# Another order table and an uneven split of the last tile in a fused attention and feed-forward kernel

## The chip, the cores and the metric

The kernel runs on one core of one Trainium2 chip. The metric is the device time of one execution in microseconds (us); lower is better. The core's engines have queues of their own: TensorE (PE) multiplies matrices, VectorE (DVE) and ScalarE (ACT) do elementwise work and empty the accumulation banks, GpSimd (POOL) here starts the loads, and SyncE (SP) starts the transposing DMAs and the stores. Each engine works its instructions off in the order in which they were written and waits for other engines by semaphores.

## The reference

Two stages, joined. A linear attention with a learned feature map, and a feed-forward layer with a squared ReLU over its output:

```python
def phi(x):                      # x: 8 batches, 8 heads, 576 tokens, 64 wide
    proj = einsum('bhsd,df->bhsf', x, w_phi)            # 64 -> 128 features
    proj = proj - max(abs(proj), axis=-1, keepdims=True)
    return concatenate([exp(proj), exp(-proj)], axis=-1)
q_p, k_p = phi(q), phi(k)
kv = einsum('bhsf,bhsd->bhfd', k_p, v);  z = sum(k_p, axis=2)
num = einsum('bhsf,bhfd->bhsd', q_p, kv)
den = einsum('bhsf,bhf->bhs', q_p, z)[..., None] + 1e-06
x = (num / den).transpose(0, 2, 1, 3).reshape(4608, 512)
h = maximum(x @ w_in, 0)                                # 512 -> 2048
out = (h * h) @ w_out                                   # 2048 -> 512
```

Inputs and output are float32; the kernel multiplies in bf16.

## The kernel before

The 4608 tokens are 36 tiles of 128. A batch gives four full tiles and 64 rows that share a tile with the next batch's. The feed-forward part works in 20 chunks: four of one tile, then sixteen of two (`CHUNKS`).

For every batch the kernel

- loads k, q and v with POOL's DMAs, which cast to bf16: a main part and a rest part each (L504, L514; in pieces at the start, L507 and L525),
- turns k and q, so that the 64 features of a head lie on the partitions. Batches 0 and 1 do it on PE (L661, L856) with copies out of the banks by ACT or DVE (L456, L458). Later batches do it by transposing DMAs that SP issues: main of 16 blocks at L594, rest of 2 blocks at L598,
- projects k (L690) and q (L891, L900) on PE, takes row maxima on DVE (L627, L937) and exponentials on ACT (L635, L930), and multiplies v with a row scale (L776),
- sums up kv and z on PE (L791, L796), copies them out (kvs), and computes numerator and denominator (num/den, L984, L992); DVE adds up the pieces (L1016, L1018), and divides (L1055), which gives xo,
- turns xo into xT: on PE and by a copy in batches 0 and 1, by SP's transposing DMAs after that (L1078 for a full tile, L1081 for half a shared one).

For every chunk follow the up-projection (hp, L1143, four groups of matmuls for each tile of a chunk), ReLU (hr, L1161 on ACT or L1163 on DVE), square (sq, L1171 or L1173), down-projection (op, L1199, four parts of four matmuls for each tile), a copy of the result to SBUF (ot, L456 or L458) and a store by SP (L1221, L1224). The last tile is computed, copied and stored in two halves of 256 columns each.

The order of all this is not the order of the loops. The loops only create 2034 numbered operations. `ORDER`, a table found by a search outside of the kernel, lists their numbers in the order in which they are written to the engines; a minus sign puts an operation that two engines can do on its second one. `Plan.order()` walks the table and hands out the slots of the buffers (eight PSUM banks, two slots for each of kin, qin, vin, kT and qT, five for xT, and so on); an operation that takes a slot waits for those that read it before. `WARM` says in front of which operations PE runs filler matmuls, in units of 128 columns. Figures such as the "out" and "out2" prices in `WIRE` were used by the search alone and emit nothing.

Three waits matter below. The transposing DMA of a batch's q can be issued once the slot of qT that it overwrites is free, that is after the last projection of the q two batches before. POOL holds the loads of a batch until the main transposes of k and q of the batch before have landed: it copies one element of each (`seen`, L1240). And a chunk's up-projection waits until the xT of all its tiles has landed.

The numbers of a few operations: 864 is the last projection of batch 4's q, with a projection of k in the same operation; 857 is a num/den step; 852 and 862 issue the two transposes of x for chunk 12, 1100 and 1102 the main and rest transposes of q for batch 6; 1683 is a store; 1723 is the first up-projection of chunk 12.

Of the kernel before, what the change touches and what calls it, by code (L numbers as in the profile page):

```python
# [120 lines left out]
)  # L121


WARM = {46: 14, 48: 2, 56: 10, 63: 3, 70: 9, 77: 36, 84: 2, 133: 34, 137: 24, 147: 10, 155: 3}


class Slots:
# [128 lines left out]
def kernel(  # L256
# [14 lines left out]
    DM, DF = moe_w_in.shape  # L271
# [7 lines left out]
    NT = B * S // P  # L279
# [25 lines left out]
    plan = Plan()  # L305
# [875 lines left out]
    def op_chunk(c):  # L1181
        hst, sq, o_h2 = h2_ops[c]
        t0 = sum(CHUNKS[:c])
        for tt in range(CHUNKS[c]):

            wide = DM // 2 if t0 + tt == NT - 1 else DM
            for c0 in range(0, DM, wide):
# [3 lines left out]
                for qu in range(OPN):  # L1191
                    key = O_KEY[c][OPN * tt + qu]
# [98 lines left out]
```

## Time and profile before

| | before |
|---|---|
| median of 3 runs | 358.52 us (358.02 to 358.96) |
| profiled execution | 357.22 us |
| span of its trace | 355.4 us |
| PE busy | 345.2 us, 97% |
| DVE busy | 299.0 us, 84% |
| ACT busy | 273.2 us, 77% |
| POOL busy | 61.4 us, 17% |

The span runs from the first to the last instruction of the trace; the time of the execution has some overhead around it. In the rows that follow, a group of instructions is named by its line, engine, operation and the tiles it writes and reads; a row of a timeline gives start, length, engine, and what ended the idle time before it. A row of the windows gives busy time and number of instructions of each engine within a stretch of the span, the clock granted to PE (1.00 is full), the busy share of the DMA engines and their rate. SPq rows are issues by SP's queue; a DMA's row in the chain gives its time from issue to landing.

### The profile page before, as it was taken

What the parts mean: (1) busy time and instruction counts of PE and PEld (TensorE: products, weight loads), DVE (VectorE), ACT (ScalarE), POOL (GpSimd) and SP (SyncE); (2) the same over time, 40 slices, a digit from 0 to 9 for tenths busy, and PEclk for the clock granted to TensorE, in tenths of its full rate; (3) what the DMA queues carried; (4) which work ended last, traced back from release to release, by engine and by line L of the source; (5) the groups of instructions that cost most, each with busy time, mean ns of one, the idle gap of its engine ahead of it and who ended that gap; (6) DMA issues with size and microseconds to landing.
All of it is one profiled execution on the core that took longest, in us unless ns stands there. A gap on an engine that the chain in (4) does not pass through costs nothing.

```text
span 355.4 us, 9650 instructions
## 1 busy us (share of the span) xinstructions
PE 345.2 (97%) x3910; PEld 239.5 (67%) x3910; DVE 299.0 (84%) x669; ACT 273.2 (77%) x604; POOL 61.4 (17%) x99
## 2 busy tenths in 40 slices
PE   8889999999999999999999969999999999999996
PEld 4469678676858585758685856666865767686474
DVE  6899989999999997779997978989996999759040
ACT  5998998798889869797889976688859698282061
POOL 9634250705200070004200330000000000000000
PEclk9999999999999999999999999999999999999999
DMA  8999999999992699339972599153203020210401
GB/s 130 185 200 203 195 207 175 137 184 145 110 163 75 111 146 183 91 62 153 163 107 77 93 192 141 30 92 81 48 15 120 18 74 10 54 46 0 120 30 59
DMA packets 92203, 39.31 MB, mean 111 GB/s; under 512 B 59712, under 2 KB 87680, under 8 KB 92160
## 3 DMA queue, kind: packets, MB, share of 16 engines
q0 software_dynamic: 42752, 18.09, 43.4%
q1 hardware_dynamic: 49408, 20.62, 28.2%
q8 instruction: 30, 0.49, 0.6%
q14 instruction: 13, 0.11, 0.1%
HBM read 36.73 MB, written 9.44 MB: 130 GB/s over the span
## 4 chain that ended last, share of the span: by engine, by line
PE 86%; DMA 4%; ACT 3%; DVE 3%; POOL 1%; issue 1%; POOLq 0%; DVEq 0%
PE bk L1199 34%; PE bk L1143 34%; PE bk L984 4%; PE bk L796 4%; PE bk L891 3%; DMA xT<-xo 2%; DMA vin<-in_v_dram 2%; PE bk L690 2%; PE bk L900 2%; ACT qph L930 1%; DVE va L776 1%; PE bk L791 1%; ACT kph L635 1%; PE bk L992 1%; DVE var L766 1%; DVE m L627 1%
## 5 line engine op out<-in xcount | busy, mean ns | idle before, releaser
L1143 PE MATMUL bk<-xT,win 128*128 128x256 bf16 (+1 forms) x1280 | 135.8, 262 | 2.9 <-DMA xT<-xo 2.8
L1199 PE MATMUL bk<-wout,h 128*128 128x512 bf16 (+1 forms) x592 | 135.5, 374 | 0.0
L1143 PEld LDWEIGHTS <-win 128*128 128x128 bf16 x1280 | 112.5, 98 | 19.3 <-DMA xT<-xo 3.0
L930 ACT ACTIVATE qph<-bk 128x512 bf16<-128x512 f32 (+1 forms) x160 | 80.5, 564 | 14.4 <-PE bk L900 14.4
L1199 PEld LDWEIGHTS <-h 128*128 128x128 bf16 x592 | 53.9, 98 | 53.6 <-issue 0.6
L635 ACT ACTIVATE kph<-bk 128x512 bf16<-128x512 f32 (+1 forms) x160 | 82.0, 577 | 7.4 <-PE bk L690 7.1
L1161 ACT ACTIVATE hr<-bk 128x512 bf16<-128x512 f32 x96 | 57.6, 604 | 26.2 <-PE bk L1143 24.2
L937 DVE TENSOR_REDUCE mq<-bk 128x4 f32<-128x512 f32 (+1 forms) x80 | 48.5, 628 | 6.1 <-PE bk L891 5.9
L627 DVE TENSOR_REDUCE m<-bk 128x4 f32<-128x512 f32 (+1 forms) x80 | 48.2, 629 | 3.0 <-PE bk L690 2.3
L1171 ACT ACTIVATE h<-hr 128x512 bf16<-128x512 bf16 x72 | 45.2, 640 | 2.3 <-DVE hr L1163 1.8
L776 DVE TENSOR_TENSOR va<-vin,em 128x512 bf16<-128x512 bf16 x64 | 41.0, 684 | 0.9 <-DMA vin<-in_v_dram 0.7
L1163 DVE TENSOR_SCALAR hr<-bk 128x512 bf16<-128x512 f32 x48 | 32.8, 686 | 6.2 <-PE bk L1143 5.7
L1173 DVE TENSOR_TENSOR h<-hr 128x512 bf16<-128x512 bf16 x72 | 29.7, 418 | 8.8 <-ACT hr L1161 8.4
L456 ACT ACTIVATE ot<-bk 128x512 f32<-128x512 f32 (+1 forms) x25 | 14.8, 593 | 23.0 <-PE bk L1199 22.9
L984 PEld LDWEIGHTS <-qph 128*128 128x128 bf16 x512 | 22.2, 98 | 7.2 <-issue 1.2
L1016 DVE TENSOR_TENSOR tmp<-bk,tmp 128x260 f32<-128x260 f32 x64 | 24.9, 418 | 1.0 <-PE bk L984 0.6
L1018 DVE TENSOR_TENSOR tmp<-bk,e 128x260 f32<-128x260 f32 x62 | 23.7, 417 | 1.9 <-PE bk L984 1.2
L984 PE MATMUL bk<-kvs,qph 128*128 128x65 bf16 x512 | 24.7, 194 | 0.4 <-DVE mq L937 0.2
L1055 DVE TENSOR_TENSOR xo<-tmp,rden 128x512 bf16<-128x512 f32 (+1 forms) x39 | 24.6, 630 | 0.4
L796 PE MATMUL bk<-va,kph 128*128 128x65 bf16 x512 | 21.4, 194 | 0.0
L796 PEld LDWEIGHTS <-kph 128*128 128x128 bf16 x512 | 20.1, 98 | 1.1 <-issue 0.3
L891 PEld LDWEIGHTS <-qT 64*128 64x128 bf16 x288 | 8.7, 94 | 12.1 <-issue 10.5
(70 smaller groups left out, 267.1 us busy)
## 6 DMA issues: line engine op xcount, KB each, us to landing
out_dram<-ot SPq DMA_DIRECT2D x31, 256.0 KB, 2.5
vin<-in_v_dram POOLq DMA_DIRECT2D x8, 512.0 KB, 9.6
kin<-in_k_dram POOLq DMA_DIRECT2D x7, 512.0 KB, 8.2
qin<-in_q_dram POOLq DMA_DIRECT2D x7, 512.0 KB, 10.9
win<-in_moe_w_in_dram POOLq DMA_DIRECT2D x4, 512.0 KB, 12.3
wout<-in_moe_w_out_dram POOLq DMA_DIRECT2D x2, 1024.0 KB, 15.8
out_dram<-ot SPq DMA_DIRECT2D x10, 128.0 KB, 2.4
xT<-xo SPq DMA_TRANSPOSE x36, 2.5
```

Source lines behind the costliest of these rows:

```text
L627: nc.vector.tensor_reduce(out=st["m"].rearrange("p (n c) -> p c n", c=2)[:, par, n0 : n0 + n], in_=st["pj", g, par][:, :n], axis=AX.X, op= ...
L635: nc.scalar.activation(out=st["kph"][:, s, n0 : n0 + n, par], in_=st["pj", g, par][:, :n], func=ACT.Exp, scale=1.0 - 2.0 * s)
L776: nc.vector.tensor_tensor(out=st["va"][:, s, gs, 0:D], in0=tiles["v", b].rearrange("p h i d -> p (h i) d")[:, gs, :], in1=st["em"][:, s, g ...
L796: nc.tensor.matmul(out=kv[:, at + n, :], lhsT=st["kph"][:, s, 2 * h + i // 2, i % 2, :], rhs=st["va"][:, s, h * NI + i, :], start=False, s ...
L930: nc.scalar.activation(out=of_bank(st["qph", pt][:, s], bank), in_=st["pq", pt, pi][bank][:, :w], func=ACT.Exp, scale=1.0 - 2.0 * s)
L937: nc.vector.tensor_reduce(out=of_bank(st["mq", pt], bank), in_=st["pm", pt, pi][bank][:, :w], axis=AX.X, op=ALU.max, apply_absolute_value= ...
L984: nc.tensor.matmul(out=st["nd", pt, half, s, ab or n // 4][:, n % 4, :], lhsT=qph[:, s, half, sl, :], rhs=kvs[:, s, sum_of(sl), :], start= ...
L1143: nc.tensor.matmul(out=hp[:, mi, :], lhsT=win[:, kc, mc * P : (mc + 1) * P], rhs=st_x[c][:, kc, 0:nt, :], start=kc == kcs[0] and (ab is No ...
L1161: nc.scalar.activation(out=out_, in_=in_, func=ACT.Relu)
L1163: nc.vector.tensor_scalar(out=out_, in0=in_, scalar1=0.0, scalar2=None, op0=ALU.max)
L1171: nc.scalar.activation(out=out_, in_=hr, func=ACT.Square)
L1199: nc.tensor.matmul(out=st["op"], lhsT=hst["h2"][:, mc, tt * P : (tt + 1) * P], rhs=wout[:, mc, cols], start=(mc == 0), stop=(mc == KC2 - 1))
```

## The change

`ORDER` and `WARM` are replaced by the result of another search, in which transposed k and q had to be ready a small reserve, and transposed x a larger one, ahead of their first use. The operations are the same 2034 up to the last tile's, and 179 of them are on another engine than before. The last tile is computed in a part of 384 columns and one of 128, in place of two of 256. The condition for the label "out" is rewritten so that the 384 columns have it.

```diff
 ORDER = (
...
-    917, 845, 847, 846, 915, 1680, 848, 849, 864, 850, 851, 1685, 865, 1100, 869, 922, 1677, 868, 1681, 870, 866,
-    923, -1686, 924, 1688, 921, 852, 867, -1687, 919, 1682, 857, 1691, 1689, 1102, 859, 858, 925, 1694, -1690, 860,
-    928, 1683, 871, 1692, 1697, 861, 1695, 1693, 920, 862, 1700, 1696, 1698, 927, 1103, 1703, -1699, 926, 931, 1701,
...
+    836, 1673, 837, 839, 838, 916, 1674, 840, 818, 842, 841, 1678, -1675, 917, 828, 913, 918, 854, 1676, 857, 843,
+    1679, 914, 855, 856, 915, 844, 858, 847, 859, 1680, 845, 846, 1681, 848, 849, 860, 1677, 850, 864, 861, 1682,
+    1685, 1100, 920, 922, 865, 867, 923, 1688, 919, 924, 851, 1686, 1691, 925, 1102, 870, -1687, 926, -1689, 871,
+    1694, 869, 1692, 852, 929, -1690, 1697, 935, 1695, 862, 927, 1700, -1693, 1698, 931, 1703, -1696, 930, 1683,
...
 )
-WARM = {46: 14, 48: 2, 56: 10, 63: 3, 70: 9, 77: 36, 84: 2, 133: 34, 137: 24, 147: 10, 155: 3}
+WARM = {46: 14, 54: 5, 56: 10, 63: 3, 70: 43, 77: 8, 84: 2, 133: 23, 137: 24, 147: 12, 171: 1}
...
-            wide = DM // 2 if t0 + tt == NT - 1 else DM
-            for c0 in range(0, DM, wide):
+            for c0, wide in [(0, 3 * DM // 4), (3 * DM // 4, DM // 4)] if t0 + tt == NT - 1 else [(0, DM)]:
...
-                plan.issue("hw", 1 + two, key, {"sp": (1.1, 1.1) if two else (0.4, 0.4)}, e_out, "out" if wide == DM else "out2", [o_ot],
+                plan.issue("hw", 1 + two, key, {"sp": (1.1, 1.1) if two else (0.4, 0.4)}, e_out, "out" if wide > DM // 2 else "out2", [o_ot],
```

The lines shown of `ORDER` are those around 864 and the transposes of q for batch 6 and of x for chunk 12. In SP's queue the issues there stand in the order 1100, 852, 1102, 1683, 862 before and 1100, 1102, 852, 862, 1683 after.

197 rows, old and new, of the table ORDER are left out of this document.

## The prediction

> **What bounds the kernel now.** I read the busy table first, then what TensorE (PE) waits for, then the same thing by stretches of the span, then the chain that ended last around the one long wait. The page's totals, and the one long entry among PE's waits (total us, times, longest):
>
> ```profile
> span 355.4 us, 9650 instructions
> PE 345.2 (97%) x3910; PEld 239.5 (67%) x3910; DVE 299.0 (84%) x669; ACT 273.2 (77%) x604; POOL 61.4 (17%) x99
> ...
> PE bk L1143 <- DMA xT<-xo: 2.8, 1, 2.8
> ```
>
> PE is busy for 345.2 of 355.4 us and xT stalled it once, for 2.8 us. The windows show where PE was not busy.
>
> ```profile
> core 0: us, PE busy (x) PEld busy (x) DVE busy (x) ACT busy (x) POOL busy (x), PEclk, DMA share, GB/s
> 15.00:20.00 5.00, 4.41 (x50) 2.64 (x49) 4.94 (x11) 4.46 (x14) 2.75 (x5) 1.00 1.40 199
> 20.00:27.70 7.70, 6.52 (x126) 4.86 (x124) 7.41 (x19) 7.47 (x20) 3.77 (x7) 1.00 1.40 198
> 27.70:208.00 180.30, 180.00 (x2194) 128.50 (x2193) 167.13 (x377) 158.30 (x355) 41.03 (x65) 1.00 0.96 140
> 208.00:211.00 3.00, 0.18 (x7) 0.06 (x2) 2.66 (x6) 1.48 (x4) 1.89 (x3) 1.00 1.60 169
> 345.10:352.30 7.20, 7.14 (x50) 4.62 (x48) 1.12 (x2) 1.62 (x4) 0.00 (x0) 1.00 0.15 55
> 352.30:355.40 3.10, 0.00 (x0) 0.00 (x0) 0.00 (x0) 0.36 (x1) 0.00 (x0) 1.00 0.12 42
> ```
>
> Until 27.70 no engine has much to spare: VectorE (DVE) is busy 4.94 of 5.00 and 7.41 of 7.70 us, ScalarE (ACT) 7.47 of 7.70. From 27.70 to 208 PE runs without loss and DVE is at 167.13 of 180.30, 93%. Then comes the hole of three microseconds, and the end costs 3.1 us after the last matmul. The granted clock is 1.00 in every window. So time can come from three places only: the start, the hole, the tail; and what the table moves elsewhere is hidden unless it makes a new hole.
>
> The hole, in the chain of waits:
>
> ```profile
> 202.97 8.00 DMA xT<-xo
> ...
> 211.02 1.05 PE bk L1143 x8
> ```
>
> The second transposed x of chunk 12 is issued at 202.97, lands 8.00 us later, and PE starts 0.05 us after that. The transposes of x usually land much faster (DMA to landing, 36 of them):
>
> ```profile
> DMA to landing us min/median/max: 2.3/2.5/8.9
> ```
>
> **The change, part 1: chunk 12.** The old order gives PE 8.65 us of work between the last num/den matmuls feeding this x (they end at 199.35, in the PE rows below) and the chunk's first up-projection, which is due at 208.0. The new order puts two up-projection groups, four down-projection groups, two kv groups and two num/den groups more between the same two operations: 8.65 + 6 x 0.88 + 2 x 0.60 + 2 x 0.25 = 15.6 (0.88 is 205.07 to 205.95, and eight matmuls of 256 columns take the same; the other two are read off below). Were the chain from producer to PE's start unchanged (199.35 to 211.02, 11.67 us), the hole would vanish. But the new order also moves x in SyncE's queue. The rows of that queue, with the two of POOL that start batch 7's loads:
>
> ```profile
> 196.38 1.91 SPq L594 DMA_TRANSPOSE qT<-qin  x1
> 198.39 1.65 SPq L1078 DMA_TRANSPOSE xT<-xo  x1
> 200.14 2.12 SPq L598 DMA_TRANSPOSE qT<-qrest  x1
> 202.35 0.53 SPq L1224 DMA_DIRECT2D out_dram<-ot  x1
> 202.97 1.89 SPq L1078 DMA_TRANSPOSE xT<-xo  x1
> ...
> 200.81 0.34 POOL L1240 COPY seen<-qT 1x1 bf16<-1x1 bf16 x1 [20.20 <-DMA qT<-qin]
> 201.27 0.90 POOL L504 DMA_DIRECT2D kin<-in_k_dram  x1
> ```
>
> The old queue has q main, x, q rest, out, x. The new one has q main, q rest, x, x, out. So neither x leaves before both transposes of q, and q main can leave only when the batch 4 projections have freed the q slot. In the PE rows those projections end at 196.32, just ahead of q main's issue at 196.38:
>
> ```profile
> 196.11 0.28 PE L690 MATMUL bk<-w,kT 64*128 64x128 bf16 x4
> 196.32 1.05 PE L1143 MATMUL bk<-xT,win 128*128 128x256 bf16 x8
> ...
> 198.94 0.41 PE L984 MATMUL bk<-kvs,qph 128*128 128x65 bf16 x8
> 199.19 5.40 PE L1143 MATMUL bk<-xT,win 128*128 128x256 bf16 x48
> ...
> 205.07 1.04 PE L1199 MATMUL bk<-wout,h 128*128 128x512 bf16 x4
> 205.95 0.22 PE L791 MATMUL bk<-var,kph 128*128 128x130 bf16 x1
> ...
> 206.55 1.03 PE L1199 MATMUL bk<-wout,h 128*128 128x512 bf16 x4
> ...
> 211.02 1.05 PE L1143 MATMUL bk<-xT,win 128*128 128x256 bf16 x8 [2.83 <-DMA xT<-xo]
> ```
>
> The real reserve is therefore counted from that release. Before: 196.32 to about 208.0, 11.68 us of PE work. After, between the same projections and the same chunk, the order has the same eight up- and three down-projection groups, two kv groups more (205.95 to 206.55, 0.60 each) and one num/den group less (198.94 to 199.19, 0.25): 11.68 + 1.20 - 0.25 = 12.63. On the old clock PE now wants x at 196.32 + 12.63 = 208.95. The queue delivers: q main 196.38, plus 1.91, 2.12 and 1.65 of issues with 0.10 between them, puts the second x at 202.36, only 0.61 earlier than before. With the same 8.00 and 0.05 it starts PE at 210.41, a wait of 1.46 us. Bounds: with the longest landing, 8.9, 2.36; if it lands at 210.97 as before, because batch 7's loads set the time and these still follow the landing of q main, 2.07; with the median landing, none. The 256 KB store that went out ahead of x now follows it, which should shorten the landing somewhat. I take a wait of 1.2, nearest to the 1.46 of the same transfer: the term is 1.2 - 2.83 = **-1.6** (-2.8 to -0.5).
>
> The Trainium skill's "DMA: Bandwidth & Descriptors", section "Queues, rings and completion order", says that a DMA engine takes turns between the queues it has work for, packet by packet. By that an x sharing with one load would take about twice 2.5 us, some 5 by estimate; the 8.00 of this trace is longer, so the row decides here, and the fair share stands below as a rival.
>
> **Part 2: the start.** Copies change engine. Up to the first up-projection DVE takes over w's copy, two casts of k, two copies of qT and two of kvs, and gives up one of xT and one of qT, each of 256 columns:
>
> ```profile
> L458 DVE CAST kvs<-bk 128x260 bf16<-128x260 f32 x11 | 4.6, 420 | 2.2 <-PE bk L796 2.2
> L458 DVE COPY qT<-bk 128x512 bf16<-128x512 bf16 x2 | 0.7, 414 | 0.0
> L458 DVE COPY xT<-bk 128x256 bf16<-128x256 bf16 x3 | 0.8, 280 | 0.0
> L458 DVE CAST kin<-h 128x256 bf16<-128x256 f32 x1 | 0.3, 295 | 0.0
> L458 DVE CAST w<-bk 128x128 bf16<-128x128 f32 x1 | 0.3, 291 | 0.8 <-PE bk L405 0.8
> ```
>
> That is 0.29 + 2 x 0.295 + 2 x 0.414 + 2 x 0.42 - 2 x 0.28 = 2.0 us more for DVE, on an engine that was 97% busy from 15 to 27.7; ACT loses more than it gains. The fillers in front of PE's operations are shifted and stay about as many (147 to 145 units of 128 columns); PE has idle time for them there. Bounds: +2.0 if DVE sets the start throughout; -0.6 if ACT does (PE lost 0.59 from 15 to 20). The first copies fall while DVE awaits loads, the others where it is full: **+0.6**.
>
> **Part 3: the middle.** Counted the same way over the rest, DVE gets about 2 us more; the cover is the 13 us that DVE had free between 27.70 and 208. The other chunks' reserves for x grow or stay ample, and none waited before (the one entry among PE's waits). A spot where DVE was already late may cost a few tenths: **+0.1** (0 to +0.8).
>
> **Part 4: the tail.** The last tile's 32 matmuls of 256 columns become 16 of 384 and 16 of 128.
>
> ```profile
> 27.74 1.05 PE L1143 MATMUL bk<-xT,win 128*128 128x128 bf16 x16
> 28.63 0.28 PE L856 MATMUL bk<-ident,qrest 128*128 128x128 bf16 x2
> ...
> L456 ACT ACTIVATE ot<-bk 128x256 f32<-128x256 f32 x2 | 0.8, 384 | 2.5 <-PE bk L1199 2.5
> ...
> out_dram<-ot SPq DMA_DIRECT2D x31, 256.0 KB, 2.5
> out_dram<-ot SPq DMA_DIRECT2D x10, 128.0 KB, 2.4
> ```
>
> From 27.74 to 28.63 sixteen of 128 take 0.89, 56 ns each; four of 512 take 0.88 (205.07 to 205.95), 220 each, and 256 about half of it, so 384 is about 165: 16 x (165 + 56) = 3.54 us against 32 x 110 = 3.52. No difference. The copy after the last matmul goes from 384 ns on ACT to about 291 on DVE (w's row), and the last store from 128 to 64 KB, by the step between the two rows 0.1 less: **-0.2** (-0.4 to +0.4, if 128 columns run slower here). The Trainium skill's "TensorE: Matmul & The Clock Gate", section "Back-to-back issue gap", gives about 81 ns for 128 columns in a stream of weight loads and matmuls, by which the tail would gain 0.4 less; the row of 56 ns contradicts it.
>
> **Sum.** -1.6 + 0.6 + 0.1 - 0.2 = -1.1. The profiled execution took 357.22, 1.8 us beside its span and 1.3 below the median of 358.52; it would take 356.1, and the median becomes 357.4. What a measurement here can tell from no change is 0.3%, 1.08 us, so the forecast lies right at that bound.
>
> **Rivals.** (a) The fair share: x lands within 6.5 us and the hole is gone. For: the median of 2.5, the store no longer ahead. Against: 8.00 in the same place. The Trainium skill's "DMA: Bandwidth & Descriptors" is the page whose rule would give it. -2.83 + 0.6 + 0.1 - 0.2 = -2.3, 356.2. (b) No gain: DVE sets the start and all of 2.0 appears. For: 4.94 of 5.00. Against: ACT is as full from 20 on and is relieved. -1.6 + 2.0 + 0.1 - 0.2 = +0.3, 358.8. (c) Slower: the queue holds x longer than the reserve grew. The transposes of q do not always issue in 1.91:
>
> ```profile
> L594 SPq DMA_TRANSPOSE qT<-qin x6: 1841/2430/3527, 57.7 to 236.5; - x6
> ```
>
> With 3.53 and a landing of 8.9 the wait is 1.46 + 1.62 + 0.9 = 3.98, 1.15 above the old; with the other terms +1.65, 360.2. The term turns into a loss once x lands over 9.4 us after 202.36. For: both x stand behind both q. Against: 1.91 is near the minimum of that row, in this very place. (d) More than that: (a) and a start that gains its 0.6, 355.0.
>
> **Chances and range.** Forecast 0.50 (its own range 356.3 to 358.4), (a) 0.17, (b) 0.15, (c) 0.13, (d) 0.05. Leaving out (c) and (d), 0.18, gives 355.8 to 359.4. Faster by over 1.08 us: (a), (d) and 0.28 of the forecast, 0.50; within: 0.22 of the forecast and 0.13 of (b), 0.35; slower: (c) and 0.02 of (b), 0.15.
>
> **What the new profile would show.** Part 1: SyncE's rows with both q transposes ahead of both x, the second x some 6 us after q main, and a PE wait on xT at chunk 12 of 1 to 2 us; none says (a), 3 or more (c). Part 2: the first row of L1143 with 128 columns, at 27.74 now, and PE's idle time up to 41 us; later by 2 says (b). Part 3: no other entry among PE's waits above half a microsecond. Part 4: the last down-projection to the end in about 0.2 us less. The prediction is wrong if a chunk other than 12 waits for x, or if the wait there is set by something that the old trace does not show.

## The result, and the profile after

The changed kernel takes 353.5 us (median of 4 executions, 353.32 to 354.35) against 358.52 us (358.02 to 358.96): a ratio of 0.9865, 95% interval 0.9844 to 0.9885. That is 5.0 us less, where 1.1 was forecast and 355.8 was the lower end of the range. The two profiled executions are only 2.9 us apart, 354.35 and 357.22: the one of before happened to be among its kernel's shorter ones, the one of after its kernel's longest. Both halves of this, the 2.9 and the other 2.1, need a reason.

The page of the changed kernel, and PE's waits in it (total us, times, longest):

```profile
span 352.6 us, 9652 instructions
PE 345.7 (98%) x3908; PEld 238.8 (68%) x3908; DVE 302.1 (86%) x678; ACT 268.9 (76%) x594; POOL 63.2 (18%) x100
...
PE bk L432 <- DVE zero L425: 1.0, 1, 1.0
PE bk L791 <- DVE mq L937: 0.6, 1, 0.6
PE bk L1095 <- DVE xo L1059: 0.4, 1, 0.4
```

PE is as busy as before, in a span 2.8 us shorter, and no wait for xT is left. The windows of the changed kernel say the same by stretches; the one around chunk 12 is the third:

```profile
core 0: us, PE busy (x) PEld busy (x) DVE busy (x) ACT busy (x) POOL busy (x), PEclk, DMA share, GB/s
0.00:27.70 27.70, 24.60 (x274) 13.98 (x274) 23.75 (x55) 20.30 (x51) 18.40 (x32) 1.00 1.21 170
27.70:204.00 176.30, 175.92 (x2128) 125.07 (x2127) 165.44 (x376) 151.16 (x337) 37.99 (x59) 1.00 0.95 139
204.00:212.00 8.00, 8.00 (x125) 5.85 (x124) 7.73 (x16) 7.01 (x20) 6.22 (x9) 1.00 0.99 140
212.00:342.00 130.00, 130.00 (x1340) 89.35 (x1335) 102.75 (x229) 88.79 (x186) 0.61 (x1) 1.00 0.32 66
```

SyncE's queue at chunk 12 has the order that was foretold, q main, q rest, both x, the store. POOL's rows are what was not:

```profile
198.24 1.93 SPq L594 DMA_TRANSPOSE qT<-qin  x1
200.27 1.61 SPq L598 DMA_TRANSPOSE qT<-qrest  x1
201.97 2.98 SPq L1078 DMA_TRANSPOSE xT<-xo  x2
205.04 0.53 SPq L1223 DMA_DIRECT2D out_dram<-ot  x1
...
204.26 0.43 POOL L1239 COPY seen<-qT 1x1 bf16<-1x1 bf16 x1 [25.91 <-DMA qT<-qin]
204.72 0.90 POOL L504 DMA_DIRECT2D kin<-in_k_dram  x1
...
DMA to landing us min/median/max: 2.5/2.7/3.0
```

The second x is issued at 203.69 (201.97 plus the first one's 1.67 and a gap) and the first load of batch 7 at 204.72. Before, that load came first, at 201.27, and the x at 202.97. The last line is the landing of the two x of chunk 12: 2.5 and 3.0 us in place of 8.00. PE begins the chunk, the last of these rows, without a wait; the first row is the one behind the projections that free the q slot:

```profile
198.17 6.29 PE L1143 MATMUL bk<-xT,win 128*128 128x256 bf16 x56
...
210.62 0.41 PE L796 MATMUL bk<-va,kph 128*128 128x65 bf16 x8
210.86 1.04 PE L1143 MATMUL bk<-xT,win 128*128 128x256 bf16 x8
```

The difference of the two spans can be split at the chunk's first row. Ahead of chunk 12 PE now has four down-projection matmuls of 512 columns more (0.88 us by the rows), four kv pairs of L791 and L796 more (0.30 each, as from 210.25 to 210.56 in the new trace) and two matmuls of 128 columns fewer (0.11): 2.0 us of work more. Without its wait of 2.83 the kernel before would have begun the chunk at 208.19, and with 2.0 more at 210.2; the changed kernel begins at 210.86, so it has lost 0.7 up to there. From there to the end of the last matmul it takes 138.4 us (to 349.23) against 141.2 (to 352.24), 2.9 less, 2.0 of which is the work moved: a gain of 0.9. After the last matmul it takes 3.4 against 3.2. So -2.8 for the hole, +0.7, -0.9, +0.2: -2.8.

### The profile page after: what moved, and what is told of

It reads as the page before. It is cut to its first block, busy times and chain, and to the rows that moved or that the text cites. A ratio compares the mean times of both kernels' runs of the same rounds, so it can differ in the third digit from the quotient of the medians.

```text
span 352.6 us, 9652 instructions
## 1 busy us (share of the span) xinstructions
PE 345.7 (98%) x3908; PEld 238.8 (68%) x3908; DVE 302.1 (86%) x678; ACT 268.9 (76%) x594; POOL 63.2 (18%) x100
## 4 chain that ended last, share of the span: by engine, by line
PE 94%; DVE 3%; ACT 2%; issue 0%
PE bk L1143 36%; PE bk L1198 35%; PE bk L796 4%; PE bk L984 4%; PE bk L891 3%; PE bk L690 2%; PE bk L900 2%; PE bk L432 2%; ACT kph L635 1%; PE bk L791 1%; DVE m L627 1%; PE bk L992 1%; PE bk L856 1%; PE bk L1095 1%; DVE mq L937 1%; DVE va L776 0%
## 5 line engine op out<-in xcount | busy, mean ns | idle before, releaser
L1198 PE MATMUL bk<-wout,h 128*128 128x512 bf16 (+2 forms) x592 | 135.7, 374 | 0.0
L1161 ACT ACTIVATE hr<-bk 128x512 bf16<-128x512 f32 x94 | 56.4, 601 | 20.8 <-PE bk L1143 20.2
L1171 ACT ACTIVATE h<-hr 128x512 bf16<-128x512 bf16 x73 | 46.2, 638 | 5.6 <-DVE hr L1163 4.7
L1163 DVE TENSOR_SCALAR hr<-bk 128x512 bf16<-128x512 f32 x50 | 34.1, 685 | 4.3 <-PE bk L1143 2.5
L456 ACT ACTIVATE ot<-bk 128x512 f32<-128x512 f32 (+1 forms) x22 | 13.3, 604 | 20.0 <-PE bk L1198 19.9
L984 PEld LDWEIGHTS <-qph 128*128 128x128 bf16 x512 | 21.4, 98 | 6.0 <-issue 1.2
L984 PE MATMUL bk<-kvs,qph 128*128 128x65 bf16 x512 | 23.8, 194 | 0.5 <-DVE mq L937 0.3
L796 PE MATMUL bk<-va,kph 128*128 128x65 bf16 x512 | 21.3, 194 | 0.0
L796 PEld LDWEIGHTS <-kph 128*128 128x128 bf16 x512 | 20.1, 98 | 1.1 <-issue 0.2
L458 DVE COPY ot<-bk 128x512 f32<-128x512 f32 (+1 forms) x15 | 9.9, 661 | 9.4 <-PE bk L1198 9.3
```

The lines of the kernel that those rows point to most:

```text
L796: nc.tensor.matmul(out=kv[:, at + n, :], lhsT=st["kph"][:, s, 2 * h + i // 2, i % 2, :], rhs=st["va"][:, s, h * NI + i, :], start=False, s ...
L984: nc.tensor.matmul(out=st["nd", pt, half, s, ab or n // 4][:, n % 4, :], lhsT=qph[:, s, half, sl, :], rhs=kvs[:, s, sum_of(sl), :], start= ...
L1161: nc.scalar.activation(out=out_, in_=in_, func=ACT.Relu)
L1163: nc.vector.tensor_scalar(out=out_, in0=in_, scalar1=0.0, scalar2=None, op0=ALU.max)
L1171: nc.scalar.activation(out=out_, in_=hr, func=ACT.Square)
L1198: nc.tensor.matmul(out=st["op"], lhsT=hst["h2"][:, mc, tt * P : (tt + 1) * P], rhs=wout[:, mc, cols], start=(mc == 0), stop=(mc == KC2 - 1))
```

## The experiments

**A second trace of the kernel before.** No edit.

> The kernel before, unchanged, for a second trace. If the hole at chunk 12 is the same in every execution, PE waits for xT between 2.5 and 3.1 us there again and the span is 355 to 356. If the hole varies with how the transfers fall (which would explain that the profiled execution was 1.3 us below the median), the wait differs from 2.83 by 1 us or more and the span moves by as much.

It took 358.82 us, with a span of 357.0, longer than the 355 to 356 expected with the same wait. The wait is the same:

```profile
PE bk L1143 <- DMA xT<-xo: 2.9, 1, 2.9
```

but what follows the hole is not. The windows of this second trace, around the hole:

```profile
205.00:208.00 3.00, 3.00 (x49) 1.98 (x44) 3.00 (x6) 3.00 (x9) 0.63 (x2) 1.00 1.41 213
208.00:211.00 3.00, 0.19 (x7) 0.07 (x3) 2.68 (x6) 1.49 (x4) 1.87 (x3) 0.99 1.50 191
211.00:212.00 1.00, 0.90 (x5) 0.65 (x6) 0.00 (x0) 0.00 (x0) 0.26 (x1) 0.50 1.58 185
212.00:213.00 1.00, 1.00 (x8) 0.75 (x7) 0.00 (x0) 0.00 (x0) 0.00 (x0) 0.50 1.58 185
213.00:214.00 1.00, 1.00 (x20) 1.00 (x19) 0.00 (x0) 0.97 (x3) 0.00 (x0) 0.50 1.31 174
214.00:215.00 1.00, 1.00 (x23) 0.97 (x21) 0.52 (x2) 0.29 (x1) 0.00 (x0) 0.83 1.65 88
...
211.10 1.89 PE L1143 MATMUL bk<-xT,win 128*128 128x256 bf16 x8 [2.91 <-DMA xT<-xo]
```

The granted clock (the seventh figure) is at 0.50 when PE starts again at 211.10 and stays there for some 3.2 us; the first eight matmuls of chunk 12 take 1.89 us instead of 1.05. At half clock those 3.2 us hold 1.6 us of work less. In the trace that the prediction was made from, the same windows have 1.00. So the hole costs 2.9 us in some executions and about 4.5 in others.

The mean granted clock that is on record for every execution bears this out. In the four sets of executions of the kernel before that came with these experiments, each on another chip, 25 have a clock of 1.0 and 34 one of 0.995, which is what 3.4 us at a half come to. Their medians are 357.1 and 358.7 us in the first set, then 356.6 and 358.3, 357.3 and 358.7, 357.1 and 358.7: the lower clock goes with 1.4 to 1.7 us. Where in the span it fell, only a trace can show.

Why one hole brings the clock down and another does not can be argued from two traces. In all fourteen traces the stretches between two changes of the clock are whole multiples of 3.41 us long (204.80 and 3.41 in this one; 351.57 in the first trace, from 4.25 to 355.82). Counted in such steps, the hole nearly fills one step in this trace (first row) and straddles two in the first trace (the other rows):

```profile
207.51:210.92 3.41, 0.68 (x19) 0.56 (x17) 3.17 (x7) 1.98 (x5) 1.79 (x3) 1.00 1.47 212
...
205.64:209.05 3.41, 2.54 (x43) 1.74 (x40) 3.41 (x7) 3.41 (x10) 0.00 (x0) 1.00 1.56 208
209.05:212.46 3.41, 1.44 (x25) 1.35 (x26) 1.61 (x4) 0.79 (x2) 2.14 (x3) 1.00 1.51 170
```

How little work in a step is too little, these two do not tell. The Trainium skill's "TensorE: Matmul & The Clock Gate", section "What's actually happening", has the clock at a half after an idle window of some 3.4 us that runs freely, not from the kernel's start; a hole of 2.9 that brings the clock down in one execution and not in another agrees in kind, though the hole is shorter than that figure.

**The loads held back, old table.** POOL also waits for both x of chunk 12 before the loads of batch 7:

```diff
                 for n, name in enumerate("kq"):
                     nc.gpsimd.tensor_copy(out=seen[0:1, n : n + 1], in_=turned[name, b - 1][1][name + "T"][0:1, 0, 0:1])
+                if b == 7:
+                    for u in range(2):
+                        nc.gpsimd.tensor_copy(out=seen[0:1, u : u + 1], in_=st_x[12][0:1, 0, u, 0:1])
```

> The old table, but POOL also waits for both transposes of x for chunk 12 before it starts the loads of batch 7 (it copies one element of each). If these loads make the transpose take 8.0 us, it lands in 2.5 to 4.5, PE's wait there goes from 2.8 to 0 and the time falls by about 2.8 us (0.992); the loads start some 4 us later and nothing waits for them. If the store and the transposes on SyncE's own queue make it slow, it still takes over 6 us, the wait stays above 1 us and the time falls by 1.5 us at most.

354.12 us (353.96 to 354.95), 0.9893 of the kernel before (0.9869 to 0.9917). SyncE's and POOL's rows:

```profile
202.24 0.53 SPq L1224 DMA_DIRECT2D out_dram<-ot  x1
202.86 1.22 SPq L1078 DMA_TRANSPOSE xT<-xo  x1
...
205.50 0.41 POOL L1243 COPY seen<-xT 1x1 bf16<-1x1 bf16 x1 [2.32 <-DMA xT<-xo]
205.95 0.90 POOL L504 DMA_DIRECT2D kin<-in_k_dram  x1
```

The x leaves SyncE as late as before (202.86, behind the store and the q transposes) and lands by 205.5: 2.5 us, not 8.0. The loads of batch 7, and nothing on SyncE's own queue, made it slow. The gain, 3.7 us by medians, is more than the wait of 2.8: none of the six executions has the lower clock, and against the seven of the kernel before on this chip that do not have it either (median 357.1) the gain is 3.0. Three more lines in the old table give as much as the new table with the old tail on the same chip (354.18, below).

**The hole filled.** In the old table, 12 fillers of 512 columns ahead of the first up-projection of chunk 12, in the bank that it overwrites:

```diff
                     kcs = range(KC1) if ab is None else (ab, ab + 2)
+                    for _ in range(12 if c == 12 and mcs[0] == 0 else 0):
+                        nc.tensor.matmul(out=hp, lhsT=zero, rhs=zero.unsqueeze(1).to_broadcast([P, 4, P]), start=True, stop=True)
```

> The old table, with 12 filler matmuls of 512 columns (some 2.6 us) in front of the first up-projection of chunk 12; they write the bank that the real matmuls overwrite and do not wait for x. The hole is as long as before, but PE is busy in it. If a hole of 3 us lets the clock fall to a half afterwards in some executions (as in the second trace of the kernel before) and this makes the spread of 356.1 to 359.4, the executions now lie within 0.8 us of each other, near 356.5 to 357.2, and their median is 0.5 to 1.5 us below that of the kernel before. If the spread has another source, it and the median of about 358 stay.

357.09 us (356.61 to 358.58, 12 executions) against 358.18 (355.75 to 359.48, 17), a ratio of 0.9987 (0.9965 to 1.0008). The interval includes 1, but the clocks on record decide: none of the twelve has the lower clock, while eleven of the seventeen of the kernel before have it (358.02 to 359.48; the other six take 355.75 to 357.03). The three longest of the twelve, 357.71, 358.42 and 358.58, have spans of 355.8, 355.6 and 355.4 us, close to the others' 354.8 to 355.5; what makes them long is 1.9 to 3.2 us outside the span, in place of 1.7 to 2.0. So PE, kept busy in the hole, kept its clock, and the upper group of the kernel before is the one with the lower clock. The median stays 0.5 us above those six: x landed 8.3 us after its issue, and PE still waited 0.5 us for it behind the fillers.

**The new table with SyncE's old order.** Two numbers of the new table moved, nothing else:

```diff
-    1685, 1100, 920, 922, 865, 867, 923, 1688, 919, 924, 851, 1686, 1691, 925, 1102, 870, -1687, 926, -1689, 871,
-    1694, 869, 1692, 852, 929, -1690, 1697, 935, 1695, 862, 927, 1700, -1693, 1698, 931, 1703, -1696, 930, 1683,
+    1685, 1100, 920, 922, 865, 867, 923, 1688, 919, 924, 851, 1686, 1691, 925, 870, -1687, 926, -1689, 871,
+    1694, 869, 1692, 852, 1102, 929, -1690, 1697, 935, 1695, 927, 1700, -1693, 1698, 931, 1703, -1696, 930, 1683, 862,
```

> The new table, but with SyncE's queue at chunk 12 as in the old one: q main, x, q rest, store, x. Nothing else moves. Theory A, the queue's order saved the second x, which now leaves before the loads of batch 7 begin: with the old order q main lands sooner, the loads begin sooner, the second x leaves after them, takes some 8 us again and PE waits 1.5 to 2.5 us at chunk 12; the time rises by 1.5 to 4 us over the changed kernel (some 355 to 357.5). Theory B, the larger reserve of PE work was enough by itself: no wait at chunk 12, and the time of the changed kernel.

354.04 us (353.55 to 354.38), no wait at chunk 12. Theory A was wrong as put: with the old order q main still landed 5.8 us after its issue, the first load came at 204.48, and the second x, issued at 203.94, was ahead of it all the same and landed in 2.6 us. As x was never behind the loads here, theory B is not shown either. The next run puts it there.

**The new table with x behind the loads.** A four-byte copy on SyncE that reads what POOL writes just before the loads:

```diff
-    1694, 869, 1692, 852, 929, -1690, 1697, 935, 1695, 862, 927, 1700, -1693, 1698, 931, 1703, -1696, 930, 1683,
-    1103, 868, -1701, 1709, -1699, 1101, 1188, 1189, 1704, 932, 1706, 921, 1702, 1191, -1705, 933, 1710, 866, 1707,
+    1694, 869, 1692, 852, 929, -1690, 1697, 935, 1695, 927, 1700, -1693, 1698, 931, 1703, -1696, 930, 1683,
+    1103, 868, -1701, 1709, -1699, 1101, 1188, 1189, 862, 1704, 932, 1706, 921, 1702, 1191, -1705, 933, 1710, 866, 1707,
...
+    behind = consts.tile([1, 2], BF16)
...
+                            if c == 12 and u == 1:
+                                nc.sync.dma_start(out=behind, in_=seen)
```

> The new table, but SyncE holds the second x of chunk 12 until the loads of batch 7 begin: a four-byte copy of what POOL writes just before them stands ahead of it (and the x stands behind the store). It should leave some 0.7 us after the first load, at about 205.3, 1.6 us later than in the changed kernel. If the order against the loads decides, it takes 7 to 9 us instead of 2.5, lands at 212.5 to 214, PE waits 1.6 to 3.2 us at chunk 12, and the median rises by 2 to 5 us over the changed kernel, more than the wait where the clock falls afterwards. If the larger reserve is enough whatever the transfer collides with, it lands by 210.9, PE does not wait and the time stays within 0.5 us of the changed kernel.

355.96 us (355.02 to 357.7), 0.9942 of the kernel before (0.9923 to 0.9962); the changed kernel on the same chip (below) 0.9892 (0.9868 to 0.9916). The rows:

```profile
204.84 0.75 SPq L1079 DMA_DIRECT2D behind<-seen  x1
205.65 1.22 SPq L1081 DMA_TRANSPOSE xT<-xo  x1
...
212.37 1.03 PE L1146 MATMUL bk<-xT,win 128*128 128x256 bf16 x8 [1.21 <-DMA xT<-xo]
```

Issued at 205.65, 2.0 us later than in the changed kernel, x lands 6.6 us after that, and PE waits 1.2. PE was ready at 211.16, so a transfer of 2.5 us could have left as late as 208.6 without a wait. Landing, wait (1.2) and median (1.7 us over the changed kernel) all fell short of the ranges expected for this case, but on its side. So the larger reserve does not cover a transfer among the loads; what removed the hole is that x leaves ahead of them.

**The changed kernel again,** on the chip of the last run.

> The changed kernel, unchanged, on the same chip as the two above. With no hole it has no lower clock: its executions lie within 1.2 us of each other while those of the kernel before spread over 3 us or more; its median is 353.3 to 354.3, 0.986 to 0.990 of the kernel before.

354.24 us. Four of the six lie between 353.72 and 354.29; the other two, 355.31 and the profiled one of 356.77, have a mean clock of 0.995. The spread of 1.2 us that was expected does not hold, and the profiled execution shows the lower clock at the start:

```profile
20.00:23.00 3.00, 2.37 (x63) 2.22 (x63) 3.00 (x7) 2.78 (x8) 1.51 (x2) 1.00 1.28 206
23.00:26.00 3.00, 2.54 (x54) 1.93 (x53) 3.00 (x10) 1.85 (x6) 0.88 (x1) 1.00 1.44 194
26.00:28.00 2.00, 1.59 (x21) 1.01 (x22) 2.00 (x7) 1.69 (x5) 0.93 (x2) 1.00 1.54 196
28.00:30.00 2.00, 2.00 (x19) 1.70 (x18) 2.00 (x6) 1.67 (x4) 1.19 (x2) 0.60 1.41 200
30.00:32.00 2.00, 2.00 (x23) 2.00 (x22) 1.08 (x2) 1.56 (x4) 1.81 (x3) 0.55 1.24 208
```

After 8 us in which PE was busy for 6.5 the clock is at a half for 3.41 us (the two last rows, 0.60 and 0.55, hold these), where the first trace of the same kernel has 1.00 after 6.9 busy us in the same eight. The expectation "with no hole it has no lower clock" was wrong: it fell here without a long pause. In the step of 3.41 us ahead of the fall PE was busy for 2.6, more than the 1.44 of the step from 209.05 above, which no fall followed; so the busy time of a step alone does not decide, and what does stays open. With the executions at the lower clock left out on both sides, the change gains 3.2 us on this chip (354.14 against 357.33), in place of 3.8 with all of them.

**Why q main landed late.** In the kernel before and the variants that keep its order and engines (five traces) q main lands 4.3 us after its issue; in six traces of the new table, 5.8 to 5.9. One 16 KB packet of the instruction queue begins 4.28 to 4.49 us after the issue in the former and 3.91 to 4.07 in the latter, while the last packets of q main are under way. To shift it, seven filler matmuls were taken out of the new table at the start (the columns stay about the same):

```diff
-WARM = {46: 14, 54: 5, 56: 10, 63: 3, 70: 43, 77: 8, 84: 2, 133: 23, 137: 24, 147: 12, 171: 1}
+WARM = {46: 14, 54: 4, 56: 10, 63: 4, 70: 44, 77: 8, 84: 2, 133: 24, 137: 24, 147: 12, 171: 1}
```

> The new table with fillers 54, 63, 70 and 133 rounded to whole matmuls of 512 columns: 2 units more of filler in all, but 7 matmuls (14 PE instructions with their weight loads) fewer. In the changed kernel one 16 KB packet of the instruction queue begins at 202.27, while q main's last packets are under way, and q main lands 5.9 us after its issue; in the kernel before it begins at 200.80, after them, and q main lands after 4.3. If that packet is PE's code and holds q main up, it now begins some 0.6 us later, q main lands after 4.3 to 4.5, the loads of batch 7 begin before the second x leaves, the x takes 6 to 8 us, PE waits 0.5 to 1.5 us at chunk 12 and the median rises by 0.5 to 2.5 us. If the packet belongs to another engine, or is not what delays q main, then q main still lands after 5.7 or more, there is no wait and the time stays within 0.5 us of the changed kernel.

354.52 us (353.92 to 355.08), 0.9911 of the kernel before (0.9885 to 0.9936). The rows:

```profile
197.86 1.94 SPq L594 DMA_TRANSPOSE qT<-qin  x1
199.90 1.60 SPq L598 DMA_TRANSPOSE qT<-qrest  x1
201.59 3.23 SPq L1078 DMA_TRANSPOSE xT<-xo  x2
...
202.24 0.28 POOL L1239 COPY seen<-qT 1x1 bf16<-1x1 bf16 x1 [23.99 <-DMA qT<-qin]
202.69 0.90 POOL L504 DMA_DIRECT2D kin<-in_k_dram  x1 [0.18 <-issue]
...
DMA to landing us min/median/max: 5.6/6.8/7.9
...
211.60 1.03 PE L1143 MATMUL bk<-xT,win 128*128 128x256 bf16 x8 [0.95 <-DVE m L627]
```

q main landed after 4.3 us, the first load came at 202.69, ahead of the second x (203.56), the two x took 5.6 and 7.9 us, and PE lost 0.95 at chunk 12. (The row names a reduction on DVE, which ends at 211.51. The same reduction ends at 211.89 in the changed kernel, after the matmuls that began at 210.86, so these do not wait for it; the x, landed at 211.5, is what they waited for.) This is the forecast's case nearly to the letter: same table, x behind the loads, a wait of 0.95 where 1.2 was expected. But the reason given for the shift was wrong. The packet began 4.08 us after q main's issue, though PE had 14 instructions fewer; it was hardly moved, which speaks against PE's code, and q main landed early all the same. A turn between 4.07 and 4.08 us fits these twelve traces but not a thirteenth: in the new order with the old engines (below) the packet begins 4.22 us after q main's issue, and q main lands after 6.1. So the packet's time does not decide the landing. The run shows one thing more: its first x, issued at 201.59 and so 1.1 us ahead of the first load, took 5.6 us, not 2.5. A start one microsecond ahead of the loads is no guarantee.

**The tail alone, both ways.** The new table with the old halves, and the old table with the new split (the last tile's hunk of the diff undone, or done alone).

> The new table with the last tile in 256 and 256 columns. If the tail is worth the forecast 0.2 us, this is slower than the changed kernel by 0.2 us (0.4 to -0.4), and about 0.987 of the kernel before. If 128 columns run slower in the tail than the 56 ns of the earlier row, this is faster than the changed kernel by up to 0.4. A gain of 1 us or more for the uneven split would show as 0.990.

> The old table with the last tile in 384 and 128 columns. The forecast is 0.2 us less than before, a ratio of 0.9995, within what can be told from no change; the hole at chunk 12 stays. If the uneven split carries the gain, the ratio is below 0.995.

The first takes 354.18 us, 0.9897 of before (0.9870 to 0.9924), with a trace in which the last matmul ends at the same 349.24 as in the changed kernel and the span is 352.9 against 352.6. The second takes 357.91 against 357.86, 0.9999 (0.9977 to 1.0021). From the last matmul to the end of the span it takes 3.2 us with the old split and 2.9 with the new one in the old table, 3.7 and 3.4 in the new table. So the split is worth some 0.3 us in the traces and nothing that the times can tell; it carries none of the 5 us. Why the new table's tail is 0.5 longer with either split stays open.

**Order and engines exchanged.** The signs of one table on the order of the other.

> The new table's order with every operation on the engine that the old table gave it. If the loss of 0.8 us that the new table has up to chunk 11 comes from the work moved to VectorE, PE's lag there falls to that of the old table and the time is up to 0.8 us below the changed kernel (some 352.7 to 353.5), less what the later stages lose. If it comes from the order, the lag stays and the time is that of the changed kernel or above it.

> The old table's order with the engines of the new one. The hole at chunk 12 stays, so the time is that of the kernel before, plus up to 0.8 us if the moved copies cost time, and new waits of PE for VectorE show before chunk 6. If the engines carried part of the gain after chunk 12 (0.8 us), PE's lag from chunk 13 to 19 grows by 0.8 us less than before.

363.77 us, 1.0159 of the kernel before (1.0130 to 1.0187), and 369.48, 1.0323 (1.0288 to 1.0358). Both expectations failed: the first loses 9.7 us against the new table with SyncE's old order on the same chip (354.04), the second 11.3 against the kernel before (358.18), in many short waits of PE for both engines and, in the second, one of 2.0 for xT. The runs cannot say what the engines alone are worth; they say that an order and its engines belong together.

**The start's ten copies put back,** in the new table.

> The new table with the ten operations that the start moved to another engine (before the first up-projection) back where the old table had them. If their 2.0 us more for VectorE cost PE time, the first up-projection starts earlier than 28.01, at 27.4 to 27.8, and the time falls by 0.2 to 0.6 us. If the start is set by loads and by ScalarE, it starts at 28.0 or later and the time stays or rises.

354.61 us, 0.9901 (0.9880 to 0.9922), the same as the changed kernel on that chip, and the first up-projection stands where it stood:

```profile
27.98 2.84 PE L1143 MATMUL bk<-xT,win 128*128 128x128 bf16 x48
```

against 28.01 in the changed kernel and 27.74 before. In the other traces of the new table with the same start it begins at 27.73, 28.01, 28.03 and 28.49 (the last behind a load that came 1.06 us late), in those of the old table between 27.58 and 27.94. The ten operations on other engines do not set the start.

## Why the prediction was wrong, step by step

Two steps failed, the landing of x in part 1 and the price of the hole in the sum.

**Part 1.** The reserve counted from the release of the q slot was right (12.63 us of work; in the changed kernel the row behind those projections begins at 198.17 and the chunk at 210.86, 12.69 later), and so was the queue's order. The step that failed is the landing of 8.00 us taken over from the old trace, with its reason, "because batch 7's loads set the time and these still follow the landing of q main", taken with the landing of q main as before. q main landed 5.9 us after its issue and not 4.3, the loads began 1.0 us behind the second x and not 1.1 us ahead of it, and x took 2.5 us. The term was -2.8, not -1.6: its lower bound, which is rival (a) in outcome, but not by a fair share of the engines; the x that did run among the loads took 6.6 and 7.9 us in the two runs that put it there. Where x does run among them, the waits of 0.95 and 1.2 us are the forecast's 1.2. Which of the two cases a table falls into depends on when q main lands; that it landed late here could not be foreseen from the old trace, and no run shows its cause.

**The price of the hole** was the larger error in the median. The hole was priced at the 2.83 us of one trace, and the 1.3 us by which that execution lay below its median were carried over. The second trace shows 2.9 of wait and about 1.6 of half clock after it. Taking the hole away takes both away: with the loads held, or the hole filled, none of 18 executions has the lower clock, and holding the loads alone gained 3.7 us by medians. Even the run with seven fillers fewer, whose wait of 0.95 is what part 1 forecast, gained 3.3. The 5.0 us of the first comparison is at the upper end: its three unprofiled executions of the kernel before (358.02 to 358.96) lie above every execution of the other sets that has a clock of 1.0 (357.81 at most), and on another chip the same pair differs by 3.8. "The median becomes 357.4" would have needed the sum from a typical execution, and the typical one of the kernel before is not the one profiled.

**Part 2**, +0.6: the first up-projection came 0.27 later, within the scatter of this start (27.58 to 27.94 in the old table's traces, 27.73 to 28.49 in the new one's), and it stayed there with DVE's copies put back, so the reason given is wrong. **Part 3**, +0.1: +0.7 up to chunk 12 and -0.9 behind it (part 2 included in the former), in pieces of a few tenths that no run took apart; one new wait of 0.6 us, for a maximum on DVE, stands just above the half microsecond that the prediction allowed. Rival (b) and rival (c) did not come: no start of 2 us, and x not later but earlier. **Part 4**, -0.2: the split gave 0.3 in the traces, with no loss from the 128 columns, as the row of 56 ns had said; but with the new table's longer tail it is +0.2 from the last matmul to the end.

Open remain what delays q main in the new table, what brings the clock down without a long pause, and where the 0.9 us behind chunk 12 comes from.

## What to carry to other kernels

Before pricing a transfer by its duration in a trace, look at what was issued ahead of it: here the second transpose of x took 2.5 or 2.6 us in the three runs shown where it left 0.5 to 3.1 us ahead of a batch's loads, and 6.6 to 8.3 us where it left 0.9 to 2.1 us behind them, and a wait on the loads' side bought about as much as a new table of 2034 operations. A hole in PE can cost more than its length, through the clock behind it, and only in some executions: compare the profiled execution with the spread of the others, and with their granted clocks, before its gaps are taken as the price. A searched order and its choice of engines are one solution; half of it is worse than either whole.

## What the runs showed of the hardware that was not expected

A pause of PE of 2.9 us was followed by a granted clock of 0.50 for 3.4 us in one execution and by none in another with nearly the same pause (2.8); 34 of 59 executions of that kernel have the mean clock of such a fall, and none of 18 in which the pause was removed or filled. In the second trace of the changed kernel the clock fell after 8 us in which PE was never idle for long but busy for only 6.5. And the landing of one transposing DMA switched between 4.3 and 5.9 us with nothing in its queue changed; one table thereby had its second x ahead of the loads, and a variant that differs by seven fillers at the start did not. No run shows the cause.
